# A small FP32 product inside a fused attention and MLP kernel, cut into three one-pass products

## The chip, the cores and the metric

The kernel runs on one core of one Trainium2 chip. The metric is the device time of one execution in microseconds (us). Before the change the median of three runs is 944.46 us (944.22 to 944.83).

## The reference: what is computed

A linear attention without softmax, followed by an MLP:

```python
def _attn_ref(q, k, v, g_norm):                      # (8, 8, 576, 64): batch, heads, rows, head_dim
    kv = np.einsum('bhsd,bhse->bhde', k, v)
    out = np.einsum('bhsd,bhde->bhse', q, kv)
    rms = np.sqrt(np.mean(out * out, axis=-1, keepdims=True) + 1e-06)
    return (out / rms * g_norm).astype(np.float32)

def _moe_ref(x, w_in, w_out):                        # x: (4608, 512), w_in: 512 x 2048, w_out: 2048 x 512
    h = x @ w_in
    sp = np.maximum(h, 0.0) + np.log1p(np.exp(-np.abs(h)))
    g = h * erf(sp)
    return (g @ w_out).astype(np.float32)
```

The weights come as float64 and are converted on the chip. Results are float32.

## The kernel before

The rows are worked in nine groups `T = 0..8`: groups 0 to 7 are the first 512 rows of each batch entry, group 8 is what remains of all eight. The attention of a group is made in four head pairs `p = 0..3`: two heads of 64 fill the 128 partitions, so that their two 64x64 matrices `kv` stand on the diagonal of one 128x128 tile `bd`, and one matmul multiplies both heads' q by them.

The large products of the MLP are not done as FP32 matmuls from the third group on (and partly in the second). Each operand is cut into parts[...]: a high part, a low part, and a scaled sum of both. Two products add up in one bank (`n_ps`), the third goes to another (`m_ps`), and a combination of the two banks is the result:

```python
SHIFT = 4096.0

def upper(x, high):                                    # ScalarE
    nc.scalar.activation(high, x, AF.Copy, scale=1.0 + 2.0**-13)

def lower(x, high, low, both):                         # VectorE, two instructions
    lower_only(x, high, low)                           #   low  = x - high
    both_only(high, low, both)                         #   both = low * SHIFT + high

def lower_w(x, high, low, both):                       # VectorE, for weights
    # low = high * SHIFT - x ;  both = high - low
    ...

banks = [(ps_h, "h"), (ps_h, "h")] + [(ps_o, f"o{i}") for i in range(4)]

def product(weights, moving, turns=True):
    n_ps, m_ps = (pool.tile([P, G], FP32, name=name, tag=tag)
        for name, (pool, tag) in zip(("n_ps", "m_ps"), banks[:2]))
    if turns:                                          # the next product takes the next two of six banks
        banks.extend(banks[:2])
        del banks[:2]
    for ps, forms in ((n_ps, (0, 1)), (m_ps, (2,))):
        for k in range(4):
            for form in forms:
                nc.tensor.matmul(ps, lhsT=weights(form, k), rhs=moving(form, k), ...)
    return n_ps, m_ps
```

The attention of a head pair is a list of pieces that the MLP's loop lays between its own work. What this case is about (cut to groups 3 to 7):

```python
halves = FIRST <= T < B                                # FIRST = 2, B = 8

def products():
    kv_ps = st["kv"] = bank("kv_ps")
    ...                                                # k^T v of two heads, FP32, 10 matmuls of 64x64 each
    st["qT"] = square_tile("qT")
    for i in range(2):                                 # VectorE
        s = slice(i * D, i * D + D)
        nc.vector.tensor_copy(out=bd[s, s], in_=kv_ps[s, s])
    ...                                                # for every second p: the remaining rows of q
    qt_ps = bank("qt_ps")
    for j in range(J):
        nc.tensor.transpose(qt_ps[:, j * P : j * P + P], qs[:, j], ident)
    nc.scalar.copy(st["qT"], qt_ps)

def apply():
    qT, o_ps, kv_ps = st["qT"], bank("se_ps"), st.pop("kv")
    nc.tensor.matmul(kv_ps[:, o_tail], lhsT=bd, rhs=st.pop("tail"), start=True, stop=True)
    nc.tensor.matmul(o_ps, lhsT=bd, rhs=qT, start=True, stop=True)        # FP32, 128x512
    nc.vector.tensor_copy(out=x_last[:, p, T * R : T * R + R], in_=kv_ps[:, o_tail])
    st["o"] = o_ps
    nc.scalar.activation(qT, o_ps, AF.Square)

def halve():                                           # VectorE: sq_hi, sq_lo
    ...
def mean(table=True):                                  # TensorE: two one-pass products into ms_ps;
    ...                                                # ScalarE: table load, Ln, Exp, Square, table load
def norm():                                            # VectorE: three instructions, ms_ps and "o" to x
    ...
def split():                                           # x to its three parts
    ...
```

`bank` takes one of two PSUM banks of the attention (`ps_at`); the six others are the MLP's. The late loop, from the third group on, has four stages for each group. In a stage four hidden units are made, and the four output rows of the stage before:

```python
for m in range(first_batch, batches + 1):
    T, b = divmod(m, NB)
    todo = list(attention(T + 1, b))
    places = (0, 2, 3, 5, 6, 8)                        # others at group ends
    ...
    pieces(0)
    for i in range(BATCH):                             # 4 hidden units
        n_ps, m_ps = hidden(T, b * BATCH + i)
        ...
        if i == 0:
            for half in range(done, 2):
                g.append(cut_upper(old_h, half))       # ScalarE: g_forms
        if done <= i < 2:
            cut_lower(old_h, i, g[i])                  # VectorE: g_forms, two of 128x1024
        evacuate()                                     # ScalarE: h <- n_ps, VectorE: h += m_ps
        nc.scalar.activation(s[:, i], h[:, i], AF.Softplus)
        pieces(i + 1)
    for i in range(2):
        nc.scalar.activation(part(s, i), part(s, i), AF.Erf)
    ...
    for j in range(J):                                 # 4 output rows of the stage before
        result(T2, b2, j, g, w)
        ...                                            # after j == 1, VectorE: h *= s, in two halves
        pieces(BATCH + 1 + j)

def result(T, b, j, g, w):
    ps = product(...)
    if b == 0:
        ...
        nc.vector.tensor_scalar(out=es[j], in0=ps[0], scalar1=SHIFT - 1.0, scalar2=None, op0=ALU.mult)
    else:
        add_scaled(es[j], ps[0], SHIFT - 1.0)          # VectorE
    add(es[j], ps[1])                                  # VectorE
```

Of the kernel before, what the change touches and what calls it, by code (L numbers as in the profile page):

```python
# [39 lines left out]
FP32 = mybir.dt.float32  # L40
# [14 lines left out]
FIRST = 2  # L55
# [5 lines left out]
def kernel(  # L61
# [207 lines left out]
    def attention(T, p, pools=None):  # L269

        st = {}

        halves = FIRST <= T < B
        bd = bd_kv[:, (T * NP + p) % 2, :]

        q_tail, o_tail = slice(P, 2 * P), slice(2 * P, 2 * P + R)

        def bank(name):
            pool, tag = (pools or {}).get(name, (ps_at, "at"))
            return pool.tile([P, G], FP32, name=name, tag=tag)  # L280

        def square_tile(name):

            if T == 0:
                return gate.tile([P, G], FP32, name=name, tag="h")
            return attp.tile([P, G], FP32, name=name, tag="qT")

        def products():

            kv_ps = st["kv"] = bank("kv_ps")  # L290
            ks, vs, qs = (x.pop((T, p)) for x in (k_sb, v_sb, q_sb))
            C = chunks(T)
            for c in range(C):
                rows = slice(0, S // C + (c < S % C))
                for i in range(2):
                    s = slice(i * D, i * D + D)
                    nc.tensor.matmul(  # L297
                        kv_ps[s, s],
                        lhsT=ks[rows, i, c],
                        rhs=vs[rows, i, c],  # L300
                        start=(c == 0),
                        stop=(c == C - 1),
                    )
            if p % 2 == 0:
                nc.tensor.transpose(kv_ps[:, q_tail], q_last[:, p // 2], ident)
            if p == NP - 2:
                for i in range(NP):
                    load_last(T + 1, i)
            st["qT"] = square_tile("qT")
            for i in range(2):  # L310
                s = slice(i * D, i * D + D)
                nc.vector.tensor_copy(out=bd[s, s], in_=kv_ps[s, s])
            if p % 2 == 0:
                tails[T] = attp.tile([P, P], FP32, name="qT_last", tag="t")
                nc.vector.tensor_copy(out=tails[T], in_=kv_ps[:, q_tail])
            st["tail"] = tails[T][:, p % 2 * R : p % 2 * R + R]
            qt_ps = bank("qt_ps")
            for j in range(J):
                nc.tensor.transpose(qt_ps[:, j * P : j * P + P], qs[:, j], ident)  # L319
            nc.scalar.copy(st["qT"], qt_ps)  # L320

        def apply():
            qT, o_ps, kv_ps = st["qT"], bank("se_ps"), st.pop("kv")
            nc.tensor.matmul(kv_ps[:, o_tail], lhsT=bd, rhs=st.pop("tail"), start=True, stop=True)  # L324
            nc.tensor.matmul(o_ps, lhsT=bd, rhs=qT, start=True, stop=True)  # L325
# [4 lines that stand above are left out]
        def square():  # L330
            st["o"], st["qT"] = x_last[:, p, :], square_tile("sq")
            nc.scalar.activation(st["qT"], st["o"], AF.Square)

        def halve():
            sq = st.pop("qT")
            hi = st["hi"] = attp.tile([P, G], FP32R, name="sq_hi", tag="rms_r")
            lo = st["lo"] = attp.tile([P, G], FP32R, name="sq_lo", tag="sq_lo")
            nc.vector.tensor_copy(out=hi, in_=sq)
            nc.vector.tensor_tensor(out=lo, in0=sq, in1=hi.bitcast(FP32), op=ALU.subtract)

        def mean(table=True):
            ms = st["ms"] = bank("ms_ps")
            if halves:


                nc.tensor.matmul(ms, lhsT=mean_w, rhs=st.pop("hi"), start=True, stop=False)  # L346
                nc.tensor.matmul(ms, lhsT=mean_w, rhs=st.pop("lo"), start=False, stop=True)  # L347
                u = square_tile("u")
# [12 lines left out]
            if table and (T > 0 or p == NP - 1):  # L361
                softplus_table()

        def norm():
            ms, u, r = (st.pop(name) for name in ("ms", "u", "r"))
            nc.vector.scalar_tensor_tensor(
                out=u, in0=ms, scalar=EPS, in1=u, op0=ALU.add, op1=ALU.mult
            )
            nc.vector.scalar_tensor_tensor(
                out=u, in0=u, scalar=3.0, in1=r, op0=ALU.subtract, op1=ALU.mult  # L370
            )
            if T < FIRST:
                if T not in xT:
                    xT[T] = wide.tile([P, KC, G], FP32, name="xT", tag="ab"[T])
                x = xT[T][:, p, :]
            else:
                x = st["x"] = x_new.tile([P, G], FP32, name="x", tag="x")
            nc.vector.scalar_tensor_tensor(
                out=x,
                in0=st.pop("o"),  # L380
                scalar=gm_col,
                in1=u,
                op0=ALU.mult,
                op1=ALU.mult,
            )

        def split():
            if T >= FIRST:
                thirds(st.pop("x"), *(form[:, p] for form in x_forms[T]))

        def loads():
            load_pair(T * NP + p + 2)

        if T == 0:
            return products, apply, halve, mean, norm
        if T == B:
            return lambda: None, square, lambda: None, mean, norm, split

        pieces = ((products,), (apply,), (halve, loads)) if halves else ((products, loads), (apply,), ())
        return (*(partial(chain, *group) for group in pieces), mean, norm, split)  # L400

# [44 lines left out]

    banks = [(ps_h, "h"), (ps_h, "h")] + [(ps_o, f"o{i}") for i in range(4)]

    def product(weights, moving, turns=True):


        n_ps, m_ps = (
            pool.tile([P, G], FP32, name=name, tag=tag)
            for name, (pool, tag) in zip(("n_ps", "m_ps"), banks[:2])
        )
        if turns:
            banks.extend(banks[:2])
            del banks[:2]
        for ps, forms in ((n_ps, (0, 1)), (m_ps, (2,))):
            for k in range(4):  # L460
                for form in forms:
                    nc.tensor.matmul(  # L462
                        ps,
                        lhsT=weights(form, k),
                        rhs=moving(form, k),
                        start=(form == forms[0] and k == 0),
                        stop=(form == forms[-1] and k == 3),
                    )
        return n_ps, m_ps
# [276 lines left out]

    low_room.close()
    room.close()
    ctx.enter_context(tc.tile_pool(name="shift", bufs=1, side="right")).tile([P, 504], FP32, name="shift")
    late_r = ctx.enter_context(tc.tile_pool(name="late_r", bufs=1, side="right"))  # L750
    gate_r = ctx.enter_context(tc.tile_pool(name="gate_r", bufs=1, side="right"))
    w_out_p = ctx.enter_context(tc.tile_pool(name="w_out_p", bufs=7, side="right"))
# [13 lines left out]
    def result(T, b, j, g, w):  # L766

        ps = product(
            lambda form, f: g[j // 2][:, form, f, j % 2 * P : j % 2 * P + P],
            lambda form, f: w[f][:, form],  # L770
        )
        if b == 0:
            if j == 0:
                all_e = wide.tile([P, J, DM], FP32, name="e", tag="a")
                es.update((i, all_e[:, i]) for i in range(J))
            nc.vector.tensor_scalar(
                out=es[j], in0=ps[0], scalar1=SHIFT - 1.0, scalar2=None, op0=ALU.mult
            )
        else:
            add_scaled(es[j], ps[0], SHIFT - 1.0)  # L780
        add(es[j], ps[1])
# [5 lines left out]
    for m in range(first_batch, batches + 1):  # L787
# [21 lines left out]
                todo[5] = partial(chain, todo[5], softplus_table)  # L809
        elif b == NB - 1:  # L810
            places = (0, 2, 3, 5, 6, 7)

        def pieces(place):
            while todo and places[-len(todo)] <= place:
# [101 lines left out]
```

## Time and profile before

| | before |
|---|---|
| median of three runs | 944.46 us |
| span of the profiled execution | 942.4 us, 11743 instructions |
| TensorE busy (matmul) | 924.8 us, 98% |
| VectorE busy | 742.6 us, 79% |
| ScalarE busy | 615.6 us, 65% |
| granted TensorE clock | 0.999 |

Rows of the profile name an engine (PE is TensorE, PEld its loading of weights, DVE VectorE, ACT ScalarE), the line of the kernel, the operation, and what it writes and reads. The costliest groups that belong to the parts in question (busy us, mean ns of one, idle time ahead and who ended it):

```profile
L325 PE MATMUL se_ps<-qT,bd_kv 128*128 128x512 f32 x64 | 34.9, 628 | 0.0
L320 ACT COPY qT<-qt_ps 128x512 f32<-128x512 f32 x32 | 18.7, 584 | 34.1 <-PE qt_ps L319 34.1
L328 ACT ACTIVATE qT<-se_ps 128x512 f32<-128x512 f32 x32 | 18.6, 580 | 1.6 <-PE se_ps L325 1.6
L776 DVE TENSOR_SCALAR e<-n_ps 128x512 f32<-128x512 f32 x28 | 19.2, 686 | 14.4 <-PE n_ps L462 14.4
```

The matmul of the first line is recorded twice for each FP32 product, and a matmul's length in such a row counts its way through the array, which overlaps with the next; so the chain of work, which counts from start to start, is the view to take its cost from. A group's busy time alone doesn't say whether anything waits for it.

### The profile page before, as it was taken

To read this page: it belongs to the slowest core of one execution; us is meant where nothing else is said; L and a number is where in the kernel's file an instruction comes from. 1 tells how busy PE (TensorE), PEld (TensorE's weight loads), DVE (VectorE), ACT (ScalarE), POOL (GpSimd) and SP (SyncE) were. 2 spreads that over 40 slices of the span, in tenths; PEclk is the share of its full clock that TensorE was granted. 3 is DMA by queue.
4 is the path that set the end of the run, shared out by engine and by line. 5 is a ranking of instruction groups with operands and counts; after the bars stand their busy time and mean duration, and the time that the engine had idled before them with its cause. 6 is when DMAs were issued, how large, how long until landed. Compare 5 with 4: busy or idle time off the path is not lost.

```text
span 942.4 us, 11743 instructions
## 1 busy us (share of the span) xinstructions
PE 924.8 (98%) x4272; PEld 683.4 (73%) x4272; DVE 742.6 (79%) x1056; ACT 615.6 (65%) x825; POOL 2.4 (0%) x10
## 2 busy tenths in 40 slices
PE   6999999999999999999999999999999999999997
PEld 4444445666688888888888888888888888888886
DVE  3999858887577787877778888878887877787667
ACT  3899776776766666666666666666666666665551
POOL 1000000000000000000000000000000000000000
PEclk9999999999999999999999999999999999999999
DMA  9766406899699998998899889998896778778871
GB/s 257 276 204 207 150 1 227 318 351 335 214 363 335 309 325 283 306 311 307 280 287 314 294 298 309 311 303 296 293 325 260 263 253 345 284 286 287 353 263 46
DMA packets 111842, 259.78 MB, mean 276 GB/s; under 512 B 43864, under 2 KB 69544, under 8 KB 111784
## 3 DMA queue, kind: packets, MB, share of 16 engines
q1 hardware_dynamic: 110152, 256.73, 78.7%
q10 hardware_dynamic: 1568, 2.29, 0.8%
q8 instruction: 34, 0.56, 0.2%
q14 instruction: 24, 0.20, 0.1%
q0 software_dynamic: 64, 0.00, 0.0%
HBM read 224.40 MB, written 34.60 MB: 275 GB/s over the span
## 4 chain that ended last, share of the span: by engine, by line
PE 92%; DVE 4%; DMA 2%; ACT 1%; issue 0%; SPq 0%; DVEq 0%
PE n_ps L462 45%; PE m_ps L462 22%; PE o_ps L520 10%; PE h_ps L692 6%; PE se_ps L325 3%; PE kv_ps L297 2%; PE qt_ps L319 2%; DMA w_raw<-in_moe_w_in_dram 1%; PE ms_ps L351 1%; DMA v_sb<-in_v_dram 1%; DVE h L876 1%; DVE e L445 1%; PE ms_ps L346 1%; PE ms_ps L347 1%; PE kv_ps L324 1%; DVE e L440 0%
## 5 line engine op out<-in xcount | busy, mean ns | idle before, releaser
L462 PE MATMUL n_ps<-x_forms,w_in_parts 128*128 128x512 f32 x896 | 232.5, 401 | 0.1
L462 PE MATMUL n_ps<-w_out_parts,g_forms 128*128 128x512 f32 x928 | 231.2, 391 | 0.0
L462 PEld LDWEIGHTS n_ps<-w_out_parts,g_forms 128*128 128x128 f32 x928 | 174.2, 188 | 38.4 <-issue 1.4
L462 PEld LDWEIGHTS n_ps<-x_forms,w_in_parts 128*128 128x128 f32 x896 | 166.8, 188 | 43.1 <-issue 9.3
L852 ACT ACTIVATE s<-h 128x512 f32<-128x512 f32 x112 | 71.0, 633 | 178.9 <-DVE h L445 178.9
L445 DVE TENSOR_TENSOR h<-m_ps,h 128x512 f32<-128x512 f32 x116 | 79.7, 687 | 59.8 <-ACT h L837 43.8
L462 PE MATMUL m_ps<-w_out_parts,g_forms 128*128 128x512 f32 x464 | 124.2, 389 | 0.0
L462 PE MATMUL m_ps<-x_forms,w_in_parts 128*128 128x512 f32 x448 | 120.0, 390 | 0.0
L520 PE MATMUL o_ps<-w_out_sb,h_sb 128*128 128x512 f32 x224 | 100.8, 593 | 0.3 <-DVE h_sb L642 0.3
L462 PEld LDWEIGHTS m_ps<-w_out_parts,g_forms 128*128 128x128 f32 x464 | 87.1, 188 | 18.0
L462 PEld LDWEIGHTS m_ps<-x_forms,w_in_parts 128*128 128x128 f32 x448 | 84.1, 188 | 17.7
L445 DVE TENSOR_TENSOR e<-m_ps,e 128x512 f32<-128x512 f32 x116 | 80.2, 692 | 18.2 <-PE m_ps L462 10.9
L440 DVE SCALAR_TENSOR_TENSOR e<-n_ps,e 128x512 f32<-128x512 f32 x88 | 60.3, 685 | 39.2 <-PE n_ps L462 39.2
L520 PEld LDWEIGHTS o_ps<-w_out_sb,h_sb 128*128 128x128 f32 x224 | 42.3, 190 | 48.9 <-issue 46.6
L411 DVE SCALAR_TENSOR_TENSOR g_forms<-g_forms 128x1024 fp32r<-128x1024 f32 x58 | 71.1, 1225 | 2.0
L408 DVE TENSOR_TENSOR g_forms<-h,g_forms 128x1024 fp32r<-128x1024 f32 x58 | 70.6, 1217 | 1.7 <-ACT g_forms L405 1.4
L876 DVE TENSOR_TENSOR h<-h,s 128x1024 f32<-128x1024 f32 x58 | 68.3, 1218 | 0.7 <-ACT s L856 0.7
L837 ACT ACTIVATE h<-n_ps 128x512 f32<-128x512 f32 x112 | 65.5, 585 | 3.4 <-PE n_ps L462 3.4
L405 ACT ACTIVATE g_forms<-h 128x1024 fp32r<-128x1024 f32 x58 | 58.9, 1059 | 12.2 <-PE m_ps L462 8.7
L692 PE MATMUL h_ps<-xT,w_in_sb 128*128 128x512 f32 x144 | 64.9, 594 | 0.7 <-DVE w_in_sb L240 0.6
L106 ACT ACT_TABLE_LOAD x44 | 56.5, 1283 | 0.8
L856 ACT ACTIVATE s<-s 128x1024 f32<-128x1024 f32 x56 | 56.2, 1052 | 0.3
(98 smaller groups left out, 1013.3 us busy)
## 6 DMA issues: line engine op xcount, KB each, us to landing
w_out_parts<-w_out SPq DMA_DIRECT2D x116, 768.0 KB
w_in_parts<-w_in SPq DMA_DIRECT2D x112, 768.0 KB
w_in<-w_new SPq DMA_DIRECT2D x16, 768.0 KB
q_sb<-in_q_dram SPq DMA_DIRECT2D x32, 256.0 KB
w_raw<-in_moe_w_out_dram SPq DMA_DIRECT2D x8, 1024.0 KB
out_dram<-e SPq DMA_DIRECT2D x32, 256.0 KB
k_sb<-in_k_dram SPq DMA_DIRECT2D x28, 287.5 KB
v_sb<-in_v_dram SPq DMA_DIRECT2D x28, 287.5 KB
```

What stands on the lines that cost most here:

```text
L106: nc.scalar.preload_act_table_set("softplus")
L405: nc.scalar.activation(high, x, AF.Copy, scale=1.0 + 2.0**-13)
L408: nc.vector.tensor_tensor(out=low, in0=x, in1=high.bitcast(FP32), op=ALU.subtract)
L411: nc.vector.scalar_tensor_tensor(out=both, in0=low.bitcast(FP32), scalar=SHIFT, in1=high.bitcast(FP32), op0=ALU.mult, op1=ALU.add,)
L440: nc.vector.scalar_tensor_tensor(out=out_, in0=ps, scalar=scale, in1=out_, op0=ALU.mult, op1=ALU.add)
L445: nc.vector.tensor_tensor(out=out_, in0=ps, in1=out_, op=ALU.add)
L462: nc.tensor.matmul(ps, lhsT=weights(form, k), rhs=moving(form, k), start=(form == forms[0] and k == 0), stop=(form == forms[-1] and k == 3),)
L520: nc.tensor.matmul(o_ps[j], lhsT=g[:, j * P : j * P + P], rhs=w_out_sb[:, f, :], start=(f == 0), stop=last,)
L692: nc.tensor.matmul(plain[i], lhsT=w_in_sb[:, c, i % FC * P : i % FC * P + P], rhs=xT[T][:, c, :], start=(c == 0), stop=(c == KC - 1),)
L837: nc.scalar.activation(h[:, i], n_ps, AF.Copy, scale=SHIFT - 1.0)
L852: nc.scalar.activation(s[:, i], h[:, i], AF.Softplus)
L876: nc.vector.tensor_tensor(out=part(h, half), in0=part(h, half), in1=part(s, half), op=ALU.mult)
```

## The change

It replaces the one FP32 product of `apply` by three one-pass products of parts, for groups 3 to 7, which is 20 head pairs. It is for TensorE, which has one product of full precision less to do. The parts of q are cut from the transposes while they lie in PSUM, the parts of the kv tile from `bd`. The result takes two of the MLP's six banks in turn in place of an attention bank, and is put together in SBUF (`o`), where the normalization reads it later. The scaling of a first output row goes from VectorE to ScalarE, a piece `cut` is put in at place 1 of the stage (after the first hidden unit), and a tile that was only there to shift addresses gives its place to the kv parts.

```diff
         halves = FIRST <= T < B
+        parts = FIRST < T < B
...
             for i in range(2):
                 s = slice(i * D, i * D + D)
                 nc.vector.tensor_copy(out=bd[s, s], in_=kv_ps[s, s])
+            if parts:
+                kv = st["kv3"] = parts_p.tile([P, 3, P], FP32R, name="kv_forms", tag="kv3")
+                nc.vector.tensor_scalar(
+                    out=kv[:, 0],
+                    in0=bd,
+                    scalar1=(1.0 + 2.0**-13) / SHIFT,
+                    scalar2=None,
+                    op0=ALU.mult,
+                )
+                lower_w(bd, *(kv[:, i] for i in range(3)))
...
-            nc.scalar.copy(st["qT"], qt_ps)
+            if parts:
+                x = st["q3"] = [
+                    pool.tile([P, G], FP32R, name=f"q_{name}", tag=tag)
+                    for name, pool, tag in (
+                        ("high", attp, "rms_r"),
+                        ("low", attp, "sq_lo"),
+                        ("both", x_new, "x"),
+                    )
+                ]
+                upper(qt_ps, x[0])
+                st["qt"] = qt_ps
+            else:
+                nc.scalar.copy(st["qT"], qt_ps)
+
+        def cut():
+            lower(st.pop("qt"), *st["q3"])
+
+        def apply_parts():
+            x, w, kv_ps = st.pop("q3"), st.pop("kv3"), st.pop("kv")
+            nc.tensor.matmul(kv_ps[:, o_tail], lhsT=bd, rhs=st.pop("tail"), start=True, stop=True)
+            n_ps, m_ps = two_banks()
+            for i, ps in enumerate((n_ps, n_ps, m_ps)):
+                nc.tensor.matmul(ps, lhsT=w[:, i], rhs=x[i], start=(i != 1), stop=(i != 0))
+            nc.vector.tensor_copy(out=x_last[:, p, T * R : T * R + R], in_=kv_ps[:, o_tail])
+            o = st["o"] = attp.tile([P, G], FP32, name="o", tag="qT")
+            nc.scalar.activation(o, n_ps, AF.Copy, scale=SHIFT - 1.0)
+            add(o, m_ps)
+            st["qT"] = x_new.tile([P, G], FP32, name="sq", tag="x")
+            nc.scalar.activation(st["qT"], o, AF.Square)
...
+        if parts:
+            return products, cut, apply, partial(chain, halve, loads), mean, norm, split
...
-    ctx.enter_context(tc.tile_pool(name="shift", bufs=1, side="right")).tile([P, 504], FP32, name="shift")
+    parts_p = ctx.enter_context(tc.tile_pool(name="parts_p", bufs=1, side="right"))
...
         if b == 0:
...
-            nc.vector.tensor_scalar(
-                out=es[j], in0=ps[0], scalar1=SHIFT - 1.0, scalar2=None, op0=ALU.mult
-            )
+            nc.scalar.activation(es[j], ps[0], AF.Copy, scale=SHIFT - 1.0)
...
+        if len(todo) > len(places):
+            places = (places[0], 1, *places[1:])
```

Cut: the tiles `u` and `x` of the normalization share one buffer for these groups, and `two_banks` is taken out of `product`, whose text is otherwise the same.

More of the change, by code (lines that the diff above doesn't have):

```diff
@@ L308, in products @@
                     load_last(T + 1, i)
-            st["qT"] = square_tile("qT")
+            if not parts:
+                st["qT"] = square_tile("qT")
             for i in range(2):
@@ L319, in products @@
                 nc.tensor.transpose(qt_ps[:, j * P : j * P + P], qs[:, j], ident)
-            nc.scalar.copy(st["qT"], qt_ps)
+            if parts:
[25 more added lines that the diff above has]
+            nc.scalar.activation(st["qT"], o, AF.Square)
         def apply():
+            if parts:
+                return apply_parts()
             qT, o_ps, kv_ps = st["qT"], bank("se_ps"), st.pop("kv")
@@ L347, in mean @@
                 nc.tensor.matmul(ms, lhsT=mean_w, rhs=st.pop("lo"), start=False, stop=True)
-                u = square_tile("u")
+                u = (
+                    x_new.tile([P, G], FP32, name="u", tag="x")
+                    if parts
+                    else square_tile("u")
+                )
             else:
@@ L375, in norm @@
                 x = xT[T][:, p, :]
+            elif parts:
+                x = st["x"] = u
             else:
@@ L397, in attention @@
             return lambda: None, square, lambda: None, mean, norm, split
+        if parts:
+            return products, cut, apply, partial(chain, halve, loads), mean, norm, split
         pieces = ((products,), (apply,), (halve, loads)) if halves else ((products, loads), (apply,), ())
@@ L447, with two_banks @@
     banks = [(ps_h, "h"), (ps_h, "h")] + [(ps_o, f"o{i}") for i in range(4)]
-    def product(weights, moving, turns=True):
-        n_ps, m_ps = (
+    def two_banks(turns=True):
+        ps = [
             pool.tile([P, G], FP32, name=name, tag=tag)
             for name, (pool, tag) in zip(("n_ps", "m_ps"), banks[:2])
-        )
+        ]
         if turns:
@@ L458, in product @@
             del banks[:2]
+        return ps
+    def product(weights, moving, turns=True):
+        n_ps, m_ps = two_banks(turns)
         for ps, forms in ((n_ps, (0, 1)), (m_ps, (2,))):
@@ L775, in result @@
                 es.update((i, all_e[:, i]) for i in range(J))
-            nc.vector.tensor_scalar(
-                out=es[j], in0=ps[0], scalar1=SHIFT - 1.0, scalar2=None, op0=ALU.mult
-            )
+            nc.scalar.activation(es[j], ps[0], AF.Copy, scale=SHIFT - 1.0)
         else:
```

## The prediction

> **What bounds the kernel now.** I read the page first (shares, chain), then the chain in order of time in one late stage, then the timelines of VectorE and ScalarE over the same stage, and last the busy time of one stage. The chain's sum by engine says where the end is set:
>
> ```profile
> PE 92%; DVE 4%; DMA 2%; ACT 1%; issue 0%; SPq 0%; DVEq 0%
> ```
>
> TensorE sets it. A stage of the late loop is one pass over four hidden units and the four output rows of the stage before, with one head pair of the next group's attention laid between. On TensorE it runs: kv products, transposes of q, hidden units H0 and H1, the tail and the block-diagonal product, H2, H3, output row R0, the mean, R1, R2, R3. The chain over one stage boundary (start, length, instruction):
>
> ```profile
> 516.42 1.83 PE n_ps L462 x8
> 518.25 0.91 PE m_ps L462 x4
> ...
> 524.60 0.73 PE kv_ps L297 x20
> 525.33 0.58 PE qt_ps L319 x4
> 525.92 1.85 PE n_ps L462 x8
> ...
> 531.40 0.17 PE kv_ps L324 x2
> 531.57 0.91 PE se_ps L325 x2
> ```
>
> Every piece starts where the one before it ends. The first two lines are R1, ending at 519.16; the product that the change replaces starts at 531.57, which is 12.41 us later, and takes 0.91 us. From 499.76 (kv products of the stage before) to 524.60 a stage is 24.8 us, and TensorE is never idle in it:
>
> ```profile
> 499.80:524.53 24.73, 24.73 (x127) 19.98 (x128) 19.94 (x30) 15.80 (x22) 0.00 (x0) 1.00 0.93 322
> ```
>
> Here 24.73 us of stretch hold 24.73 of TensorE, 19.94 of VectorE, 15.80 of ScalarE. So VectorE has under 5 us to spare in a stage. Where that spare time lies decides this case. VectorE's timeline over the boundary:
>
> ```profile
> 519.20 0.69 DVE L445 TENSOR_TENSOR e<-m_ps,e 128x512 f32<-128x512 f32 x1 [0.21 <-PE m_ps L462]
> 519.81 2.35 DVE L876 TENSOR_TENSOR h<-h,s 128x1024 f32<-128x1024 f32 x2
> 522.08 0.68 DVE L366 SCALAR_TENSOR_TENSOR u<-ms_ps,u 128x512 f32<-128x512 f32 x1
> ...
> 528.29 0.45 DVE L312 COPY bd_kv<-kv_ps 64x64 f32<-64x64 f32 x2
> 528.78 1.22 DVE L408 TENSOR_TENSOR g_forms<-h,g_forms 128x1024 fp32r<-128x1024 f32 x1
> ...
> 531.29 0.69 DVE L445 TENSOR_TENSOR h<-m_ps,h 128x512 f32<-128x512 f32 x1
> ...
> 536.64 0.69 DVE L445 TENSOR_TENSOR h<-m_ps,h 128x512 f32<-128x512 f32 x1 [1.54 <-ACT h L837]
> ```
>
> The bracket is the idle time ahead of an instruction. Between 519.20 and 534.9 no line has one: VectorE works without a pause from the end of R1, past the stage boundary, to beyond H1. Its free time (1.54 here, some 2.7 more in the R0 and R1 part) all lies between the product and R1. Nothing of TensorE waits for this run today, because banks come free in time.
>
> **What the Trainium skill says.** "FP8 and Floating Point Precision", TensorE Precision Notes: true FP32 takes four passes through the array. The trace agrees: 0.91 us for the 128x512 FP32 product against 0.91 for four one-pass products of the same size (m_ps x4), so 0.2275 each. "PSUM — Partial Sum Buffer", Engine vs sequencer instructions: the queues of ScalarE and VectorE are strict FIFO. The timelines agree: instructions start only in the program's order, and one that waits holds up all behind it (the h copy's add waits 1.54 us while nothing passes it). "VectorE: DVE Perf Modes", Mode 2×_2P: two-tensor FP32 operations have no doubled rate, single-source ones between SBUF have. The trace agrees: 685 to 692 ns for two-tensor forms at 128x512, 419 for the cast of sq. "TensorE: Matmul & The Clock Gate", Why this matters for your kernels: idle gaps over about 3 us may halve the array's clock. This trace, at 0.999, has no such gaps in the loop to test it.
>
> **The change part by part**, for 20 head pairs (five groups, four stages each).
>
> *Removed from TensorE*: 0.91 us, replaced by 3 x 0.2275 = 0.68. Gain 0.23 x 20 = 4.6 us, if nothing waits.
>
> *Added to VectorE, ahead of the product*: three 128x128 operations that form the weights. From 685 ns at 512 and 1222 at 1024 elements, a two-tensor operation costs 0.148 + 0.00105 per element, so 0.28 at 128; twice that and about 0.22 for the scaling (the 128x128 cast took 0.227) is 0.78 us. Then q_low, 0.69, and q_both, 0.69. By the order of the changed program, these stand behind the kv copies, and q_low behind the first g_forms pair and H0's add; none of them uses the free time after the product.
>
> *Added after the product*: on ScalarE the scaled copy of n_ps (0.58); on VectorE the add of m_ps (0.69). The Square reads the sum and stands behind that add.
>
> *Moved*: 28 scalings of the first output rows from VectorE (L776, 0.686 each) to ScalarE, only in the second stage of each group, where the block row before starts.
>
> *Ordinary stage* (three of four). VectorE's unbroken run from 519.20 to the end of H0's add at 531.98 becomes 0.78 + 0.69 longer until q_low exists: 533.45. TensorE needs it for the second of its three products at 531.57 + 0.23 = 531.80: a wait of 1.65, plus some 0.03 of signalling. The third product needs q_both, 0.69 after q_low, of which 0.23 is covered: a further 0.47. H2 then starts at about 534.43 and not at 532.48: 1.95 us late, the 0.23 already counted. Does the stage give it back? No: from H2 to R1 TensorE runs at its own pace, and VectorE's next run starts again at the end of R1. So the loop is now: VectorE's run (14.25) and TensorE's part from product to R1, in turn.
>
> ScalarE adds to it. The sum of the product is formed on VectorE behind q_both, g_forms (2.39) and H1's add, near 538.05; Square waits for it, ends near 538.7, and H2's copy, which was at about 536.0, follows near 539.3. Through H2 and H3's adds and softpluses the last one ends near 542.5; table load 1.28, two Erf 2.01, table load 1.28, Ln, Exp and Square 2.05 give 549.15. VectorE, done with the gate near 548.75, waits 0.4 for it. Ordinary stage: 1.95 + 0.4 = 2.35, say 2.4 us longer.
>
> *Second stage of a group.* The moved scalings go behind the Erf calls, and the second one behind the whole chain of the mean as well. ScalarE there, before the change:
>
> ```profile
> 491.63 2.01 ACT L856 ACTIVATE s<-s 128x1024 f32<-128x1024 f32 x2
> 493.66 1.28 ACT L103 ACT_TABLE_LOAD   x1
> ...
> 496.99 1.28 ACT L106 ACT_TABLE_LOAD   x1
> ```
>
> Between Erf's end and the end of the second load lie 1.28 + 2.05 + 1.28 = 4.6 us. With R0's copy (0.58) ahead of it and R1's own (0.58), R1's row is copied 5.8 us after Erf. On the clock of the stage above: Erf ends at 545.85, R1's add starts at 551.65, where an ordinary stage has it at 543.92 + 1.95 = 545.87. So VectorE's run starts 5.8 later. It is shorter by the scalings of R2 and R3, 2 x 0.70 = 1.4. The next product comes 4.4 later, and the stage costs 1.95 + 4.4 = 6.35. Part of the wait shows earlier, at the transposes of q: their bank is the one that the normalization reads last.
>
> *Sum*: a group is 3 x 2.4 + 6.35 = 13.55; five groups 68 us. The scalings moved in the last two groups, where no such product is, may add 1 to 3. 944.5 + 68 + 2 = 1014; I say 1014.
>
> **The rivals.**
> (1) The intended gain: VectorE keeps up and 4.6 us are saved, 940. For it speaks VectorE's 5 us of spare time per stage against 2.85 us added (0.78 + 1.38 + 0.69), which fits by sums. Against it: the place of that spare time, all behind the product, and the fixed order.
> (2) Waits at the product only, and the moved scalings harmless: 20 x about 2 = 40 us, 983. This would be so if the Erf calls come much earlier than worked out, or R1's late copy is absorbed by banks. Against it: R1's add stands ahead of the gates in VectorE's order.
> (3) Banks: the product takes one of three bank pairs, so a hidden unit or output row finds its pair again after two others and one short product. I find each pair evacuated in time except in the second stage; if not, more waits in H2 or R3, 1025 and above.
> (4) The kv bank comes free earlier, since the sum no longer stays in PSUM: the weight loader's waits for the normalization (about 0.35 us in a stage) go. They lie beside TensorE's work already, so under 0.1 us each.
>
> **Range and chances.** The terms that may be off are the 128x128 operations (0.5 to 1.0 us), ScalarE's share (0 to 1 us in ordinary stages), and the second stage (3 to 8). Together 13.55 a group may be 9 to 18, so 989 to 1034; eight times in ten 985 to 1034. Faster than before by 2% (under 925.6) is out of reach: the whole saving on TensorE is 4.6 us. Within 2% (to 963.3) needs under 1 us a stage of loss: 0.05. Slower: 0.94.
>
> **What would show it.** Right: in the list of waits, TensorE waiting for q_low about 1.6 us and for q_both about 0.5 in each of the stages, and for the normalization's read ahead of the transposes in every fourth; stages of about 27 us, every fourth near 31; VectorE without idle time from R1 to q_both, and idle some 4 us ahead of R1's add in the second stage. Wrong: if TensorE's idle time stays under 10 us in all, VectorE was not behind, and the order was read wrongly; if it waits at n_ps of hidden units for evacuated banks, rival 3 is the cause; if every fourth stage is like the others, the moved scalings were mis-sized.

## The result, and the profile after

| | before | changed |
|---|---|---|
| median | 944.42 us | 1037.28 us (1036.62 to 1044.6, four runs) |
| ratio | | 1.0997 [1.0969, 1.1025] |
| TensorE busy | 924.8 us, 98% | 969.2 us, 93% |
| VectorE busy | 742.6 us | 778.4 us |
| ScalarE busy | 615.6 us | 642.5 us |
| granted TensorE clock | 0.999 | 0.927 in the profiled execution, 0.974 to 0.975 in the three others |

The kernel is 93 us slower. The profiled execution is the one of 1044.6 us; its clock stands at 0.949 also where nothing waits, so orders and waits are read from it and times from the medians.

The chain that ended last, shares of the span by engine:

```profile
PE 55%; DVE 26%; ACT 11%; issue 5%; DMA 2%; SPq 1%; DVEq 0%; ACTq 0%
```

TensorE held 92% of the chain before; now VectorE and ScalarE hold 37%. What TensorE waited for (total us, times, longest), the lines of this case:

```profile
PE n_ps L354 <- DVE q_low L459: 40.3, 19, 2.7
PE qt_ps L331 <- DVE u L412: 9.9, 5, 2.1
...
PE m_ps L354 <- DVE q_both L462: 3.4, 15, 0.2
```

The waits are where the prediction put them: at q_low (2.1 us a time, for 1.6 foretold) in 19 of 20 stages, at q_both (0.2, for 0.5), and at the transposes of q once in each of five groups. One ordinary stage holds 25.42 us of TensorE and 21.84 of VectorE in 27.19:

```profile
610.48:637.67 27.19, 25.42 (x129) 20.27 (x128) 21.84 (x35) 16.30 (x22) 0.00 (x0) 0.95 0.78 253
```

VectorE's timeline over this stage boundary, to be held against the one from 519.20 in the prediction:

```profile
605.15 0.69 DVE L496 TENSOR_TENSOR e<-m_ps,e 128x512 f32<-128x512 f32 x1 [0.21 <-PE m_ps L517]
...
608.02 0.68 DVE L412 SCALAR_TENSOR_TENSOR u<-ms_ps,u 128x512 f32<-128x512 f32 x1
...
618.83 0.68 DVE L459 TENSOR_TENSOR q_low<-qt_ps,q_high 128x512 fp32r<-128x512 f32 x1
...
622.55 0.68 DVE L496 TENSOR_TENSOR h<-m_ps,h 128x512 f32<-128x512 f32 x1
...
624.42 0.69 DVE L496 TENSOR_TENSOR o<-m_ps,o 128x512 f32<-128x512 f32 x1 [1.05 <-ACT o L357]
626.29 0.69 DVE L496 TENSOR_TENSOR h<-m_ps,h 128x512 f32<-128x512 f32 x1 [1.18 <-ACT h L892]
...
636.21 0.69 DVE L412 SCALAR_TENSOR_TENSOR u<-ms_ps,u 128x512 f32<-128x512 f32 x1 [0.91 <-ACT u L406]
```

The run without a pause is there, as predicted, and q_low at its late end. But the brackets after it are new. VectorE, the engine that everybody seems to wait for, waits three times for ScalarE. (It also waits about 1.4 us for R1, between the last two lines; that wait is over before the third one for ScalarE begins.) ScalarE in the same stretch, and the same place before the change:

```profile
623.27 0.63 ACT L907 ACTIVATE s<-h 128x512 f32<-128x512 f32 x1 [3.20 <-DVE h L496]
623.81 0.58 ACT L357 ACTIVATE o<-n_ps 128x512 f32<-128x512 f32 x1
625.14 0.63 ACT L360 ACTIVATE sq<-o 128x512 f32<-128x512 f32 x1 [0.76 <-DVE o L496]
625.68 0.58 ACT L892 ACTIVATE h<-n_ps 128x512 f32<-128x512 f32 x1
```

```profile
535.00 0.63 ACT L852 ACTIVATE s<-h 128x512 f32<-128x512 f32 x1 [1.87 <-DVE h L445]
535.54 0.58 ACT L328 ACTIVATE qT<-se_ps 128x512 f32<-128x512 f32 x1
536.02 0.59 ACT L837 ACTIVATE h<-n_ps 128x512 f32<-128x512 f32 x1
...
545.89 0.63 ACT L360 ACTIVATE u<-rms_r 128x512 f32<-128x512 f32 x1
```

The add of H1 that this ScalarE waits for, before the change:

```profile
534.29 0.68 DVE L445 TENSOR_TENSOR h<-m_ps,h 128x512 f32<-128x512 f32 x1
```

Each waits for the other in turn: H1's add, softplus and scaled copy, sum, Square and H2's copy, H2's add, and on to Erf, the mean, and the normalization (L412), from which VectorE goes without a pause to the next H1's add. That is a closed loop, and TensorE is not in it. From one L412 to the next it is 636.21 - 608.02 = 28.19 us. In the whole trace this distance is 28.0 to 28.2 us in ordinary stages that no half clock touches and up to 28.7 in those that one does (there the end of R1 comes last at the normalization), never under 28.0, although the starts of the kv products lie 26.9 to 30.5 us apart. Before the change the same loop can be added up from the two timelines: VectorE from 522.08 to the end of H1's add at 534.97, 12.9; to H2's add at 536.64, 1.67; from there to the end of the mean's chain (ScalarE's last Square ended at 546.52), 9.9: 24.5 us, beside stages of 24.8. So the kernel before ran two loops of nearly the same length, and TensorE's, the only one that the waits show, was the longer by 0.3 us. The change took 0.23 us from that one and put on the other: 2.3 before H1's add (15.2 for 12.9, with 0.3 of it a copy that falls in every second stage), 1.4 between H1's and H2's adds (3.06 for 1.67), nothing after.

In the second stage of a group the moved scalings are seen as predicted:

```profile
543.37 1.28 ACT L103 ACT_TABLE_LOAD   x1
...
546.70 1.28 ACT L106 ACT_TABLE_LOAD   x1
547.99 1.57 ACT L831 ACTIVATE e<-n_ps 128x512 f32<-128x512 f32 x3
```

and VectorE's line behind it:

```profile
548.62 0.69 DVE L496 TENSOR_TENSOR e<-m_ps,e 128x512 f32<-128x512 f32 x1 [4.55 <-ACT e L831]
```

R1's row is copied at 547.99, behind Erf, two table loads and the mean's chain, and VectorE stands idle for 4.55 us.

Two theories went into the experiments. *Parts*: the pace is set by TensorE waiting for q_low, and what exceeds the prediction is the half clock after such waits (the prediction's loop, from R1 over VectorE to the product). *Loop*: the pace is set by the loop of VectorE and ScalarE, and TensorE's waits only show that it has time.

### The profile page after: what moved, and what is told of

Its sections match the earlier page's. It is cut to its first block, busy times and chain, and to the rows that moved or that the text cites. A ratio compares the mean times of both kernels' runs of the same rounds, so it can differ in the third digit from the quotient of the medians.

```text
span 1042.8 us, 12031 instructions
## 1 busy us (share of the span) xinstructions
PE 969.2 (93%) x4292; PEld 705.1 (68%) x4292; DVE 778.4 (75%) x1148; ACT 642.5 (62%) x873; POOL 2.4 (0%) x10
## 4 chain that ended last, share of the span: by engine, by line
PE 55%; DVE 26%; ACT 11%; issue 5%; DMA 2%; SPq 1%; DVEq 0%; ACTq 0%
PE n_ps L517 24%; PE m_ps L517 11%; PE o_ps L575 9%; PE h_ps L747 6%; DVE e L496 3%; DVE h L496 3%; DVE g_forms L459 3%; DVE h L931 3%; ACT s L911 2%; DVE e L491 2%; ACT s L907 1%; ACT L103 1%; PE kv_ps L298 1%; DVE q_both L462 1%; DVE x_forms L459 1%
## 5 line engine op out<-in xcount | busy, mean ns | idle before, releaser
L517 PE MATMUL n_ps<-x_forms,w_in_parts 128*128 128x512 f32 x896 | 242.6, 415 | 1.8 <-DVE x_forms L459 0.8
L517 PEld LDWEIGHTS n_ps<-x_forms,w_in_parts 128*128 128x128 f32 x896 | 178.4, 201 | 43.2 <-DVE x_forms L459 1.5
L517 PE MATMUL m_ps<-x_forms,w_in_parts 128*128 128x512 f32 x448 | 125.1, 402 | 0.8 <-DVE e L496 0.8
L575 PE MATMUL o_ps<-w_out_sb,h_sb 128*128 128x512 f32 x224 | 105.3, 616 | 0.0
L517 PEld LDWEIGHTS m_ps<-x_forms,w_in_parts 128*128 128x128 f32 x448 | 87.3, 195 | 21.3 <-DVE e L496 1.2
L747 PE MATMUL h_ps<-xT,w_in_sb 128*128 128x512 f32 x144 | 67.6, 617 | 0.5 <-DVE w_in_sb L240 0.5
```

The lines of the kernel that those rows point to most:

```text
L575: nc.tensor.matmul(o_ps[j], lhsT=g[:, j * P : j * P + P], rhs=w_out_sb[:, f, :], start=(f == 0), stop=last,)
L747: nc.tensor.matmul(plain[i], lhsT=w_in_sb[:, c, i % FC * P : i % FC * P + P], rhs=xT[T][:, c, :], start=(c == 0), stop=(c == KC - 1),)
```

## The experiments

Stage lengths are from one start of the kv products to the next in each run's trace; "second" is the stage that begins once R3 of the stage with the moved scalings is done, and holds the longest waits.

| run | median us | ratio to before | ordinary stages | second |
|---|---|---|---|---|
| before | 944.4 | | 24.7 to 24.8 | 24.8 |
| changed | 1037.3 | 1.0997 [1.0969, 1.1025] | 26.9 to 30.5 | 30.4 to 32.9 |
| scale_back | 1018.0 | 1.0781 [1.0765, 1.0797] | 26.9 to 30.7 | as the others |
| busy_wait | 1032.4 | 1.0933 [1.0916, 1.0949] | 28.0 to 28.3 | 31.9 |
| scale_only | 976.6 | 1.0342 [1.0324, 1.0359] | 24.7 to 24.8 | 26.3 to 27.6, and 28.0 to 28.4 in the stage ahead of it |
| late_sum | 1025.8 | 1.0857 [1.0841, 1.0873] | 27.2 to 29.2 | 31.1 to 32.7 |
| cut_first | 1032.8 | 1.0932 [1.0916, 1.0948] | 27.5 to 28.2 | 31.9 to 32.4 |
| g_late | 1028.7 | 1.0887 [1.0857, 1.0916] | 26.9 to 28.6 | 33.2 to 33.5 |
| reordered | 995.2 | 1.0532 [1.0514, 1.0549] | 26.9 to 27.2, two of 28.5 | as the others |
| parts_split | 974.0 | 1.0311 [1.0297, 1.0325] | 26.1 to 26.4 | as the others |
| load_only | 983.9 | 1.0418 [1.0404, 1.0432] | 26.6 to 27.2 | as the others |
| plain_parts | 955.5 | 1.0114 [1.0097, 1.0131] | 24.6 to 25.5 | as the others |
| plain_split | 944.3 | 1.0000 [0.9991, 1.0008] | 24.55 to 24.9 | as the others |
| plain_place | 941.4 | 0.9969 [0.9957, 0.9981] | 24.6 to 24.7 | as the others |

**scale_back**: one part undone.

```diff
-            nc.scalar.activation(es[j], ps[0], AF.Copy, scale=SHIFT - 1.0)
+            nc.vector.tensor_scalar(
+                out=es[j], in0=ps[0], scalar1=SHIFT - 1.0, scalar2=None, op0=ALU.mult
+            )
```

> The changed kernel with one part undone: the scaling of the first output rows is on VectorE again. If the moved scalings cost what the prediction says (the second stage of a group 4 us longer than the others, because R1's row is copied only after the mean's chain on ScalarE), five stages get about 4 us shorter, and half-clock stretches after their longer waits go with them: about 1017 (1010 to 1024). Rival, that they only fill ScalarE's idle time: 1037 or a little more, as VectorE has 19 us of work back.

It came to 1018.0, and the long stages are gone. The moved scalings cost 19 us of the 93.

**busy_wait**: TensorE gets something to do while it waits.

```diff
             n_ps, m_ps = two_banks()
+            for _ in range(8):
+                nc.tensor.matmul(n_ps, lhsT=w[:, 0], rhs=x[0], start=True, stop=True)
```

> The changed kernel with eight more products of q_high ahead of the first one, which all write the same bank and are overwritten: nothing is computed from them, they keep TensorE at work for 1.8 us while it waits for q_low. If the time beyond the prediction (1037 against 1014) is the clock, halved for 3.4 us after waits, the half-clock stretches mostly vanish and the time falls by 15 to 25 us, to about 1017, although TensorE has 36 us more work. Rival, that the half clock lies beside other waits, and the excess is further waits: 1037 or more.

It came to 1032.4. The half-clock stretches went from some 15 (1035 us at 0.975) to one in each group, but only 5 us were won, and every ordinary stage is 28.0 to 28.3. Without the filler, stages of 27.0 and of 28.4 to 30 take turns: a stage slowed by the half clock has the next one wait less. Something of 28.0 us stands behind both. That speaks against the half clock as the cause of the excess, and for the loop.

**scale_only**: the moved scalings alone, put into the kernel before (the diff of scale_back, reversed).

> The kernel before with one part of the change alone: the scalings of the first output rows on ScalarE. By the prediction's working, R1's add then waits for ScalarE's chain of the mean, about 5 us later than before, and the bank of the attention comes free 5 us later, so TensorE waits at the kv products of the next stage: 4 to 5 us in each of five groups, about 967 (958 to 975). Rival, that ScalarE has room for them: 944.

It came to 976.6, just above the range. In the kernel before the part costs more than in the changed one, 32 us for 19; some 28 of them lie in the five groups (28.0 and about 27.1 in place of 24.7 and 24.8), the others in the two groups after. TensorE's wait is at the kv products:

```profile
PE kv_ps L297 <- DVE u L366: 16.6, 5, 3.6
```

The releaser is the normalization, which stands behind R1's add, and that behind ScalarE. A wait is 3.3 us, not the 4 to 5 expected; a half-clock stretch after each of the five, in the next stage, brings the rest (in one such stage, 27.6 us long, TensorE waits for nothing).

**late_sum**: the hand-over between the two engines made shorter.

```diff
-            add(o, m_ps)
-            st["qT"] = x_new.tile([P, G], FP32, name="sq", tag="x")
-            nc.scalar.activation(st["qT"], o, AF.Square)
+            st["m"] = m_ps
+
+        def sum_up():
+            o = st["o"]
+            add(o, st.pop("m"))
+            ...                       # sq and Square as before
-            places = (places[0], 1, *places[1:])
+            places = (places[0], 1, 2, 3, 4, *places[3:])
```

> The changed kernel with the sum of the product and its Square one place later, and the halves one place after that: H2's copy on ScalarE no longer stands behind a Square that waits for VectorE. If ScalarE's hand-over chain is part of the loop (0.4 to 1 us in a stage), 20 stages lose 8 to 20 us: about 1024. If the wait for q_low alone sets the pace: within 3 us of 1037.

It came to 1025.8: 11.5 us less by an edit that leaves q_low where it was. Stages that no half clock touches are 27.2 to 27.5, where they were 28.0. The distance between H1's and H2's adds is back at 1.67 us, and L412 no longer waits for ScalarE: the next bound is the loop of the prediction, from q_low over the product and R1 back to VectorE.

**cut_first**: the run that tells the two theories apart.

```diff
-            places = (places[0], 1, *places[1:])
+            places = (places[0], 0, *places[1:])
```

> The changed kernel with the piece cut at place 0, so that VectorE makes q_low and q_both ahead of the first g_forms pair and of H0's add. The prediction's theory, that TensorE's wait for q_low sets the pace: the parts come 3.1 us earlier, the wait is gone, 20 x 2.1 = 42 us less, about 995. New theory, that a loop of VectorE and ScalarE alone sets it (normalization, rows, forms, H0 and H1's adds; softplus, sum, Square, H2 and H3's copies and adds, Erf, the mean's chain, normalization: 28.0 us), in which this changes the order and not the length: 1037, within 6 us, and the waits only change their place.

It came to 1032.8. Its waits of TensorE:

```profile
PE qt_ps L331 <- DVE u L412: 22.2, 5, 4.4
PE m_ps L517 <- DVE h L496: 9.0, 14, 0.7
...
PE n_ps L354 <- DVE q_low L459: 3.6, 8, 0.6
```

The wait for q_low fell from 40.3 to 3.6 us, and the kernel is 4.5 us faster. The time came back as waits for H0's and H1's adds and for the normalization. From one L412 to the next it is 28.0 us still. So moving q_low moved the wait: q_low was its place, not what set the pace.

**load_only**: the same from the other side. The kernel before, with VectorE's added work and nothing that waits for it. The product stays FP32.

```diff
+            if parts:
+                kv = parts_p.tile([P, 3, P], FP32R, name="kv_forms", tag="kv3")
+                nc.vector.tensor_scalar(out=kv[:, 0], in0=bd, scalar1=(1.0 + 2.0**-13) / SHIFT, ...)
+                lower_w(bd, *(kv[:, i] for i in range(3)))
...
+        def cut():
+            low = attp.tile([P, G], FP32R, name="q_low", tag="sq_lo")
+            both = x_new.tile([P, G], FP32R, name="q_both", tag="x")
+            lower(st["qT"], st["qT"], low, both)
```

> The kernel before, product and all waits of TensorE as they were; only VectorE's added work stands in it, at the same places: the three 128x128 weight forms and two 128x512 operations, whose results nothing reads. New theory: the kernel before already has a VectorE and ScalarE loop of 24.4 us beside TensorE's 24.8, so that 2.15 us more in it show but for 0.35: 20 x 1.8 = 36 us, about 980 (972 to 988). The prediction's theory, that time is lost where TensorE waits for the parts: nothing is waited for, 944.

It came to 983.9: 39.5 us for 2.15 us of work a stage that nobody reads. The normalization of one stage and of the next, in VectorE's timeline:

```profile
595.79 0.69 DVE L378 SCALAR_TENSOR_TENSOR u<-ms_ps,u 128x512 f32<-128x512 f32 x1 [1.89 <-ACT u L372]
...
622.43 0.69 DVE L378 SCALAR_TENSOR_TENSOR u<-ms_ps,u 128x512 f32<-128x512 f32 x1 [1.89 <-ACT u L372]
```

The loop is 26.64 us, which is 24.5 + 2.15. Even here VectorE waits 1.89 us for ScalarE in each stage, while its own work is what made the loop long. This settles it: the kernel before had 0.3 us to give, not the nearly 5 us of free VectorE time in a stage.

**g_late**: work moved out of the run and into a wait.

```diff
-            if done <= i < 2:
-                cut_lower(old_h, i, g[i])
+            if i == 0 and done == 0:
+                cut_lower(old_h, 0, g[0])
...                                          # after H1's copy, add and softplus:
+            if i == 1 and done < 2:
+                cut_lower(old_h, 1, g[1])
```

> The changed kernel with the second g_forms pair on VectorE behind H1's add in place of ahead of it, where VectorE now waits for ScalarE. New theory: H1's add comes 2.45 us earlier in the loop, the pair fills the 1.05 us of waiting ahead of the sum, and the sum starts about 0.95 us earlier: 20 x 0.95 = 19 us less, about 1018. The prediction's theory: q_low stands where it stood after the same work, 1037.

It came to 1028.7 (1024.5 to 1031.7). Ordinary stages fell by the 1.0 expected, to 26.9 to 27.2, but the second ones rose from 31.9 to 33.3 and the next after them to 28.5: there TensorE waits twice, a half-clock stretch of 6.8 us falls after it, and with the loop shorter nothing hides it. 27.0 us is near what the prediction's own loop gives without ScalarE's part (24.8 + 1.95 = 26.75), which the next run tests.

**reordered**: scale_back, late_sum and g_late at once.

> The changed kernel with three orders changed at once: scalings back on VectorE, the sum one place later, the second g_forms pair behind H1's add. New theory: the loop is 12.6 to the end of H1's add, 2.45 for the pair, H2's add near 15.9, sum near 16.6, Square and H3's copy to 17.8, H3's add 18.5, softplus 19.2, and 6.65 to the normalization: 25.8 in place of 28.0. From 1018 with the scalings back, 20 x 2.2 = 44 less: about 974. If it stays above 1000, the loop is drawn wrongly.

It came to 995.2. The loop was to be 25.8 us; stages stop at 27.0, with one wait left:

```profile
PE n_ps L354 <- DVE q_low L463: 29.9, 19, 1.7
```

With the loop out of the way, the prediction's loop is the bound, at 27.0 for the 26.75 that it gave. This wait is now real.

**parts_split**: reordered, and with cut at place 0; the second g_forms pair is split, one operation ahead of H1's add (which otherwise waits for ScalarE there) and one after it.

```diff
+            elif i == 1 and done < 2:
+                lower_only(part(old_h, 1), g[1][:, 0], g[1][:, 1])
...                                          # after H1's copy, add and softplus:
+            if i == 1 and done < 2:
+                both_only(*(g[1][:, k] for k in range(3)))
```

> The changed kernel's own parts with all reorderings: scalings on VectorE, cut at place 0, the sum one place later, the second g_forms pair split around H1's add. Neither the wait for q_low (27.0 us a stage in the reordered run) nor the holes ahead of H1's and H2's adds remain; by the working of the loop 12.0 + 1.2 + 0.7 + 1.2 + 0.6 for H2's add, sum, Square and H3's copy to 18.2, H3's add 18.9, softplus 19.55, and 6.65: 26.2. From 944, 20 x 1.4 more: about 973, still slower than before, since the parts' work alone fills VectorE. If the wait for q_low was not the pace of the reordered run: 990 or more.

It came to 974.0, stages of 26.13 or 26.35 against 26.2. The number is right, but not the path to it: VectorE's normalization no longer waits for ScalarE; the chain goes from VectorE's parts of the squares (sq_lo) over TensorE's mean and R1 back to VectorE. All orders mended, the changed kernel's parts still cost 3%.

**plain_parts**: fewer operations in place of better orders, made from the kernel before. The parts are plain (low is not scaled up); three one-pass products (type FP32R) add up in one bank. What it leaves out is the product of the two low parts.

```diff
+                kv = st["kv2"] = parts_p.tile([P, 2, P], FP32R, name="kv_forms", tag="kv2")
+                nc.vector.tensor_copy(out=kv[:, 0], in_=bd)
+                nc.vector.tensor_tensor(out=kv[:, 1], in0=bd, in1=kv[:, 0].bitcast(FP32), op=ALU.subtract)
...
+                upper(qt_ps, x[0])
+                lower_only(qt_ps, *x)
...
+                nc.tensor.matmul(o_ps, lhsT=w[:, 0], rhs=high, start=True, stop=False)
+                nc.tensor.matmul(o_ps, lhsT=w[:, 1], rhs=high, start=False, stop=False)
+                nc.tensor.matmul(o_ps, lhsT=w[:, 0], rhs=low, start=False, stop=True)
```

> Made from the kernel before: three one-pass products of plain parts (high with high, the weights' low with high, the weights' high with low) that add up in one attention bank, so that no sum of parts, no second bank, no scaled copy and no add are needed; VectorE gets 1.25 us a stage in place of 2.85. The second g_forms pair stands behind H1's add. New theory: the loop of VectorE and ScalarE is 11.7 + 2.45 + 0.2 + 0.7 + 1.15 + 0.7 + 0.65 + 6.65 = 24.2 us, less than TensorE's 24.55, so the saved 0.23 us a stage show: about 940 (937 to 943). If another wait takes its place: 945 to 960.

It came to 955.5, the "other wait" of its expectation. With q_low ahead of the forms and the second pair behind H1's add, nothing stands between H0's and H1's adds, and VectorE waits 1.18 us there for H1's copy, which ScalarE makes after H0's softplus. I had left that hole out of the sum: the loop was 25.2 to 25.4, not 24.2.

**plain_split**: plain parts with the split of parts_split.

> The plain parts with the second g_forms pair taken apart: its first operation ahead of H1's add, where VectorE waits 1.18 us for ScalarE, its second behind it, where it waits for H2's copy. New theory: both waits are filled, the loop falls from 25.3 to about 24.1 us, under TensorE's 24.55, which then shows in each stage: 940 (938 to 943). If TensorE still waits at the transposes of q for the normalization: 945 to 955.

It came to 944.3, no change, and yet TensorE waits for nothing in these stages. The chain shows where the time goes: eight hidden products in two groups, the first in an odd one (its x parts lie in a tile of the right side), the second in an even one.

```profile
354.72 1.87 PE n_ps L484 x8
```

```profile
478.67 1.81 PE n_ps L484 x8
```

**plain_place**: the place of the tiles as before.

```diff
-                kv = st["kv2"] = parts_p.tile([P, 2, P], FP32R, name="kv_forms", tag="kv2")
+                kv = st["kv2"] = parts_p.tile([P, 504], FP32R, name="kv_forms", tag="kv2")[
+                    :, : 2 * P
+                ].rearrange("p (i f) -> p i f", i=2)
```

> The plain parts, split, with one thing changed: the tile of the kv parts takes 504 floats a partition, of which 256 are used, as the tile that was only there to shift addresses did, so that all tiles of the right side lie where they lay before. In the run without it eight of 18 stages (groups whose x parts lie in a tile of the right side) run at 1.87 us for eight hidden products, the others at 1.81. If it is the address: all stages near 24.6 and 12 x 0.24 = 3 us less, 941. If it is not: 944.

It came to 941.4, 0.3% under the kernel before and clear of it by its interval. Odd and even groups now run at one pace, as they did before the change. The slower pace in odd groups, about 0.25 us a stage, is in the trace of each run whose kv parts took the place of the shift tile, the changed kernel too; there the loop hides it (28.0 to 28.2 us in odd and even groups alike). Over 416 us of the late loop TensorE is never idle, with VectorE at 85%:

```profile
276.67:693.00 416.33, 416.33 (x2159) 341.76 (x2158) 355.90 (x533) 269.10 (x357) 0.00 (x0) 1.00 0.90 306
```

Stages are 24.57 and 24.69 where they were 24.72 and 24.84, so 0.15 x 20 = 3.0 us, which is the gain. It is 0.15 and not 0.23 because the first of the three products takes 0.28 from its start to the next, the others 0.23 and 0.24.

## Why the prediction was right and wrong

*Direction and places*: right. It said that TensorE would wait at q_low, q_both and every fourth time at the transposes, that VectorE runs without a pause from R1 to q_both, and that R1's add would stand idle about 4 us behind the moved scalings. All are in the trace, 4.55 us for the last.

*The size*: 93 us for the 70 foretold, above the range's upper end of 1034. The step that failed is "ScalarE adds to it". It put the hand-over as 0.4 us on top of TensorE's wait, "VectorE, done with the gate near 548.75, waits 0.4 for it". But the chain that it added up there, from VectorE's normalization at 522.08 over H1's add, the sum "near 538.05" and H2's copy to the end of the mean's chain at 549.15, is a closed loop by itself, 27.07 us, and one term of it was too small. It had the scaled copy of n_ps ready at once. In ScalarE's order that copy stands behind H1's softplus, which waits for H1's add. So the sum does not follow H1's add directly but after softplus and copy, 1.05 us later. From the end of H1's add to the start of H2's the prediction has about 2.2 us (537.15 to 539.3), and the trace 3.06. The other two terms were right within 0.1: 15.04 from the normalization to the end of H1's add (15.05 foretold) and 9.92 from H2's add back (9.85). So the loop is 28.0 and not 27.1, and ordinary stages became 28.0 (busy_wait, cut_first) where 24.8 + 2.35 = 27.15 was foretold: 0.85 for each of three in a group. The second stage is 31.9 for 31.1. Together 3 x 0.85 + 0.8 = 3.4 a group, 17 of the 23 us. That ScalarE's hand-over has this weight is shown by late_sum (11.5 us less).

*What sets the pace*: wrong in kind, under a nearly right number. "The loop is now: VectorE's run and TensorE's part from product to R1, in turn" describes a loop that exists, and at 27.0 us (reordered) it is nearly as long as foretold, 26.75. But the longer one goes through VectorE and ScalarE alone, and it hid the other. cut_first and load_only show it; neither TensorE's wait for q_low nor the product has to be there. That the two loops lie within 1.0 us of each other, so that a sum over the wrong one came near, is luck.

*The half clock*: left out of the sum, though the page that speaks of it was named. It comes about 15 times, and filling the wait wins 5 us. The last two groups took about 4 us, in scale_only and in the changed kernel's own trace, for the 2 in the sum. So 17 + 5 + 2 = 24 us stand against the 23 between sum and result; the terms are no surer than that.

*The moved scalings*: foretold 1.95 and 4.4 in the second stage, of which the 4.4 are theirs, 22 us with 1 to 3 in the last groups; undoing them won 19.

*Rivals*: the first, 940, is refuted by the result: VectorE's spare time was there and could not be used. The second, the moved scalings harmless, is refuted by scale_back. The third, bank waits at hidden units and rows, stayed at about 2 us in all. Of the fourth, the waits of the weight loader for the normalization (9.0 us in 22 waits before) are gone from the trace as said; no gain in time can be told apart.

*The chances*: the bound of 4.6 us on TensorE's whole gain held; the version that keeps it brings 3 us, not 4.6.

## What to carry to other kernels

That one engine is busy for 98% does not say that the others have room. Before work is added to an engine, add up the longest closed loop through it, from one instruction to the same one a stage later, over every engine that it hands to: here it was 24.5 us beside stages of 24.8, with VectorE busy for only 20. The wait that shows is the place where the loop meets the bound engine, and moving the instruction that is waited for changes the place; making the loop shorter, by fewer operations or by work put into its holes, changes the time.

## What the runs showed of the hardware that was not expected

- A half-clock stretch here is 3.4 us in which TensorE's granted clock is 0.5, at times two of them in a row. In the changed kernel it came in 11 of the 12 stages whose waits of TensorE add up to 2.6 us or more, and in two of six where they add up to 1.7 to 1.9. The Trainium skill ("TensorE: Matmul & The Clock Gate", Why this matters for your kernels) warns of gaps over about 3 us; single waits of 3.3 to 3.6 us (scale_only, busy_wait) and of 4.4 us (cut_first) had it after them all 15 times, but shorter ones did it too, the longest here being 2.7 at q_low. The hidden unit after such a wait took nearly double; the next one here is already at full pace (chain of the changed kernel):

```profile
562.98 3.41 PE n_ps L517 x8
...
567.95 1.84 PE n_ps L517 x8
```

  With waits of 1.7 to 1.9 us a stage (reordered) it came in two of 18 stages, with 0.4 to 0.6 us (parts_split) in none. In the changed kernel most of it is made up by a shorter wait in the next stage; in g_late, where the other loop is shorter, it is not.
- The place of tiles alone changes the pace of one-pass products: 1.87 us for eight against 1.81, with the tiles of the right side 248 floats a partition away from where they were. The slowed ones are those that read x parts lying in such a tile, as the moving operand. Over 12 stages this fits the 3 us between plain_split and plain_place. All tiles of that side moved together; which one's address it is, and why it is slow, was not tried.
